# A later first conversion, closer conversions, three filling products and another order of banks in an attention and expert kernel

## The chip, the cores and the metric

The kernel runs on one core of one Trainium2 chip. The metric is the device time of one execution in microseconds (us). Five engines work side by side, each through its own queue in order: TensorE (PE, products), VectorE (DVE), ScalarE (ACT), GpSimd (POOL) and SyncE (SP, which here only issues DMAs). They meet by semaphores.

## What is computed

Three layers follow each other, all in float32, on 1152 tokens of 512 numbers. The reference, cut to what matters:

```python
# 1. attention, 2 batches x 8 heads, 1152 keys, 576 pooled queries
q_pool = q.reshape(B, H, S // 2, 2, D).mean(axis=3)
attn = softmax(q_pool @ k.T / sqrt(D));  x = attn @ v          # -> 1152 x 512
# 2. mixture of 8 experts, each token goes to its two best
noisy = x @ w_gate + log1p(exp(x @ w_noise)) * noise
top2 = np.argpartition(-noisy, 2, axis=1)[:, :2]               # softmax over the two
out[mask] += top2_w[mask, k, None] * (relu(x[mask] @ w1[e]) @ w2[e])
# 3. a dense layer pair, 512 -> 2048 -> 512, weights given in float64
h = x @ w_in;  g = np.where(h > 0, h, np.exp(np.minimum(h, 0)) - 1)
return (g @ w_out).astype(np.float32)
```

`w_in` and `w_out` come as float64. The chip has no float64, so the kernel turns them into float32 itself, bit by bit, in 32 pieces of 128x512 numbers.

## The kernel before

**Precision.** A product of two float32 matrices is made as three products of halves: each operand is split into a high part (rounded to the format that TensorE takes) and a low part (the rest). ACT makes the high part by a copy (`W.hi`, line 674; `xh`, line 727; `hh`, line 736), DVE or POOL the low part by a subtraction (`W.lo`, line 678; `xl`, line 728; `hl`, line 737).

**Attention (lines 171 to 386).** Eight units of two heads. The order of all steps is written out in a table of planned times, and steps that other parts of the kernel put in (`extra`, line 1034) are sorted among them. At its end stand, on PE, the transposition of the last query rows (`tl1`, line 363), which ACT copies (`tl1c`, line 367), a small product with the gate's weights (`tl2`, line 371), and on DVE the sum of its result into the gate's input (`tl2c`, line 375). PSUM has eight banks. The pool of attention has three under the tag `t` (the first that is asked for), four under `s` and one under `o`. The buffers of a tag are placed where the tag is first used, in that order, and a buffer in the next pool waits for the last reader of the bank that it takes over.

**The experts.** After attention a new PSUM pool is opened, with tags `a` (3 banks), `t` (2) and `o` (3). The first product of expert 0 for the first batch (`First.l1`, line 843, planned by `plan_first`, line 858) asks for an `a` bank first; so `a` lies on the three banks that attention had as `t`. Then each expert e has a first layer (`l1`, line 735, eight steps f of twelve products of 312 columns), a second layer (`l2t`, line 745, four steps of 24 products), and the transposition of the next expert's rows (`te`, line 726, in two pairs, `t` banks) between them. All steps are events of a `Line`: each has a planned time, the events are sorted by it, and every engine gets its instructions in that order. The planned times are no waits: an engine goes on as soon as its operands are there, but never past an instruction that waits. `V0` is the planned start of expert 0 and `D`=29.7 the planned length of one expert, so expert e starts at V0+29.7e. A step of the plan is called by its planned distance from V0 below ("at 16.5").

**A branch.** At 13.37 stands a conditional (line 559) for tokens that overflow an expert; every engine passes it, and the memory for the conversions is opened only behind it.

**Weights.** `plan_weight` (line 685) plans four loads of 512 KB on SP's queue (line 672, into six buffers), four high parts on ACT and four low parts on DVE or POOL for each half of an expert (its w1 or its w2).

**Conversions.** `plan_convert` (line 696) plans each of the 32 pieces, one every `CV[1]` from `CV[0]` on:

```python
    ln.at(t-3,load); ln.at(t,bits); ln.at(t+2,small); ln.at(t+8,store)
```

`load` (line 701) is a DMA of 512 KB on SP into one of two buffers; `bits` is four instructions on DVE (lines 705 to 708); `small` two on POOL (lines 711 and 712); `store` a DMA of 256 KB on SP (line 714) of the result to DRAM. Before, the first has bits at 16.5 and each next one 5.7 later, so the last has them at 193.2. On SP the store of conversion i stands just ahead of the load of conversion i+2, both in the same in-order queue as the loads of the experts' weights.

**The dense layers (lines 967 to 1009)** run when the experts are done, in three chunks of tokens; they read the converted weights from DRAM.

Of the kernel before, what the change touches and what calls it, by code (L numbers as in the profile page):

```python
# [4 lines left out]
FT=mybir.dt.float32; FR=mybir.dt.float32r; BF=mybir.dt.bfloat16; I32=mybir.dt.int32  # L5
# [143 lines left out]
def consts(tc, cp):  # L149
    nc=tc.nc  # L150
    c={}
    jp=cp.tile([128,128],I32,name="jp")
    nc.gpsimd.iota(jp,pattern=[[1,128]],base=0,channel_multiplier=-1)
    c['id']=cp.tile([128,128],FT,name="ident")
    nc.vector.tensor_scalar(c['id'],jp,0.0,None,op0=OP.is_equal)
    c['idr']=cp.tile([128,128],FR,name="identr")
    nc.vector.tensor_copy(c['idr'],c['id'])
    rw=c['rw']=cp.tile([128,8,80],FT,name="rw"); c['wd']=cp.tile([128,4,16],FT,name="wd")
    for r in range(2): nc.vector.tensor_copy(rw[64*r:64*r+64,:,0:64],c['id'][64*r:64*r+64,None,64*r:64*r+64].to_broadcast([64,8,64]))
    return c  # L160
# [520 lines left out]
def w2_src(w2, e, i): return ap(w2,e*512*1024+i*256*512,[[512,128],[128*512,2],[1,512]])  # L681
# [176 lines left out]
def plan_first(ln, F, pm, hp, ps, T):  # L858

    A={}  # L860
    def l1(f, b, c0=0, c1=4):
        F.l1(ps,f,b,c0,c1)
        A[b,f//3]=F.a
    for f in range(8): ln.at(T['l1']*f,l1,f,0)
    for i,n in enumerate((3,3,2)):
        ln.at(T['l1']*(3*i+n)+.02,lambda i=i,n=n: F.relu(hp,0,3*i,n,A[0,i])); ln.at(max(T['hl0']+.01*i,T['l1']*(3*i+n)+.03),lambda i=i,n=n: F.rest(0,3*i,n,A[0,i]))
    for j in range(5): ln.at(T['hot']+.001*j,F.ones,pm,j)
    for c in range(4): ln.at(T['mul']+.005*c,F.mul,ps,c); ln.at(T['mul']+.03+T['dm']*c,F.cut,hp,c)
    t=T['two']
    for f in range(3): ln.at(t+.001*f,l1,f,1,0,3)  # L870
    for f in range(3): ln.at(t+.01+.001*f,lambda f=f: (setattr(F,'a',A[1,0]),l1(f,1,3,4)))
    for f in range(3,8): ln.at(t+T['l1']*f,l1,f,1)
    for i,n in enumerate((3,3,2)):
        ln.at(t+T['l1']*(3*i+n)+.02,lambda i=i,n=n: F.relu(hp,1,3*i,n,A[1,i])); ln.at(t+T['l1']*(3*i+n)+.03,lambda i=i,n=n: F.rest(1,3*i,n,A[1,i]))
# [138 lines left out]
def build(tc, q, k, v, wg, wn, noise, w1, w2, win, wout, out):  # L1013
    nc=tc.nc
    with ExitStack() as es:
        def P1(n,b=1,st=es,**kw): return st.enter_context(tc.tile_pool(name=n,bufs=b,**kw))
        cp=P1("c"); dr=P1("dr",space=bass.MemoryType.DRAM)
        xs=dr.tile([OV0+OVN+NDUMP,512],FT,name="xs"); ys=dr.tile([NROW,512],FT,name="ys")
        ms=es.enter_context(ExitStack()); ms.enter_context(tc.manual_schedule())
        wf=[win,wout]  # L1020
        wide=win.dtype!=FT
        if wide: wf=[dr.tile([1<<20],FT,name=f"wf{i}") for i in range(2)]
        c=consts(tc,cp); g={}
        gk=P1("gk")
        scat=[]
        xe=ExitStack()
        X_=P1("X",st=xe,side="right")
        pm=P1("pm0",st=xe,side="right")
        g['ic']=pm.tile([128,HC],FT,name="icap")
        X=[X_.tile([128,5,512],FT,name=f"X{b}") for b in range(2)]  # L1030
        L=[cp.tile([128,5,16],FT,name=f"L{b}") for b in range(2)]
        F=First(tc,g,X,w1,xs,c['id'])
        gb=[]
        def extra(ps,ek,kk):
            psf=lambda: ps.tile([128,512],FT,tag="t",name="pg",bufs=TB)
            pss=lambda: ps.tile([128,1,512],FT,tag="s",name="pg",bufs=4)[:,0]
            def step():
                if not gb: gb.append(gating(tc,g,0,0,range(5),cp,gk,psf,X[0],L[0],xs,scat))
                next(gb[0],0)
            def late():  # L1040
                for b in range(2): nc.gpsimd.memset(L[b][64:128,4],0.0)
                ici=g['ic'].bitcast(I32)
                nc.gpsimd.iota(ici.rearrange("p (j n) -> p j n",j=2),pattern=[[1,2],[2,HC//2]],base=HC,channel_multiplier=0)
                nc.gpsimd.tensor_copy(g['ic'],ici)
                gate_consts(tc,cp,g)
            def swap():
                ek.close()
                F.open(P1("fw",st=xe,side="right"),kk)
            ld=lambda u: STEPS['load'][3 if u==7 else min(u,2)][0]+UU*u+.01
            ev=[(ld(2),lambda: consts2(tc,c,wg,wn)),(T0,late),(ld(3),late_loads(tc,g,cp,noise))]  # L1050
            ev+=[(ld(3+i//3),f) for i,f in enumerate(zero_fills(tc,g,cp,xs,ys))]
            ev+=[(t,step) for t in GATE]
            ev+=[(PRE['swap'],swap),(PRE['load'],F.load)]
            ev+=[((max(237.1,GATE[i+10]) if i<10 else PRE['split'])+.001*(i+1),lambda i=i: F.split(i)) for i in range(20)]
            for i in range(2): ev+=[(PRE['xt'][0]+.1*i,lambda i=i: F.xt(pss,i)),(PRE['xt'][1]+.1*i,lambda i=i: F.xh(i)),(PRE['xt'][2]+.1*i,lambda i=i: F.xl(i))]
            return ev
        attention(tc,c,X,L,q,k,v,extra,WARM)
        rp=P1("rp"); wp=P1("wp"); ps=P1("ps",space=PSUM); e2=es.enter_context(ExitStack())
        hp=P1("hp",st=e2)
        W=Weights(tc,wp,rp,1); ln=Line(); xp=Late(); cv=Late()  # L1060
        wt={}
        s1,s2=[128,4,1024],[128,8,512]
        psf=lambda: ps.tile([128,512],FT,tag="t",name="pg",bufs=2)
        gt=gating(tc,g,1,1,range(5),cp,gk,psf,X[1],L[1],xs,scat)
        for t in GT: ln.at(t,lambda: next(gt,0))
        ct=counts(tc,g,cp,psf)
        for t in CNT: ln.at(t,lambda: next(ct))
        plan_first(ln,F,pm,hp,ps,FIRST)
        V0=FIRST['two']+8*FIRST['l1']+.2-EX['l2']
        wt[0,1]=plan_weight(ln,W,s2,lambda i: w2_src(w2,0,i),2,*WP['a2'])  # L1070
        wt[1,0]=plan_weight(ln,W,s1,lambda i: w1_src(w1,1,i),1,V0+WP['b1'][0],V0+WP['b1'][1],WP['b1'][2],'vpvp')
        for i in range(4): ln.at(V0+TG+i,lambda: (next(gb[0],0),next(gt,0)))
        ln.at(V0+16,joint_tail,tc,g,cp)
        for e in range(1,9):
            t=V0+D*(e-1)
            if e>1:
                f=(lambda i,e=e: w1_src(w1,e,i)) if e<8 else (lambda i: win_src(wf[0],0,i))
                wt[e,0]=plan_weight(ln,W,s1,f,1,t+WP['1'][0],t+WP['1'][1],WP['1'][2],'vpvp',None,WP['1'][3])
            f=(lambda i,e=e: w2_src(w2,e,i)) if e<8 else (lambda i: wout_src(wf[1],0,i))
            wt[e,1]=plan_weight(ln,W,s2,f,2,t+WP['2'][0],t+WP['2'][1],WP['2'][2],'vpvv',None,WP['2'][3])  # L1080
        if wide:
            for i in range(32):
                plan_convert(ln,tc,(win,wout)[i//16],wf[i//16],i%16,cv,V0+CV[0]+CV[1]*i)
        box={}
        for e in range(8):
            plan_expert(ln,tc,e,V0+D*e,[wt.get((e,0)),wt[e,1]],c['id'],xs,ys,xp,hp,ps,None if e else Hs(F),box if e==7 else None)
        ln.run(V0+EX['l2']-.05)
        xe.close()
        if OVF: overflow(tc,g,w1,w2,xs,ys,c['id'],ps)
        W.p0.p=P1("wp0",side="right")  # L1090
        with e2:
            xp.p=P1("xp",st=e2); e3=e2.enter_context(ExitStack()); cv.p=P1("cv",st=e3,side="right")
            ln.run(V0+7*D+2)
            e3.close(); xr=P1("xr",side="right"); lp=P1("lp",st=e2)
            plan_last(ln,tc,g,V0+7*D,box,c['id'],ys,xp,hp,lp,ps)
            ln.run()
        xp=P1("xp2"); x2=P1("x2"); gp=P1("gp",2)
        ln=Line()
        wi=[wt[8,0],plan_weight(ln,W,s1,lambda i: win_src(wf[0],1,i),1,*MW[0],MW[2])]
        wo=[wt[8,1],plan_weight(ln,W,s2,lambda i: wout_src(wf[1],1,i),2,*MW[1],MW[3],last=x2)]  # L1100
        for ch in range(3):
            t=62*ch
            xt=plan_combine(ln,tc,g,ch,t-30 if ch else -2,(t-3.9,t-3.5) if ch else (-.2,-.2),c['id'],ys,xp,xr,ps,box['acc'])
            plan_moe2(ln,tc,ch,t,xt,wi,wo,out,gp,xp,ps)
        ln.run()
OVF=True; T0=20; TG=4.32; WARM=8; MW=((0,2,3),(12,14,3),'pppp','pppp'); CNT=(13.2,13.9); CV=(16.5,5.7)
PRE=dict(swap=237,load=446.2,split=446.3,xt=(581.65,582.,613.1))
GT=[0,.1,.2,.25,.26,.27,.3,.4,5.35,5.36]+[5.5+.01*i for i in range(11)]
FIRST=dict(l1=1.35,hl0=5.9,hot=5.4,mul=8.05,dm=.6,two=10.85)
WP={'a2':(-2.69,3,1.5,'vvvv',None,5.5),'b1':(5.23,9.87,3.81),'1':(-2.04,1.53,2.85,1.91),'2':(10.24,16.62,3.22,0.85)}  # L1110
# [31 lines left out]
```

## Time and profile before

| what | value |
|---|---|
| time, median of 3 runs | 814.61 us (811.88 to 817.9) |
| time of the profiled execution | 808.12 us |
| its span (first to last instruction) | 806.3 us, granted TensorE clock 0.994 |
| PE busy | 768.7 us (95%) |
| DVE busy | 560.9 us (70%) |
| ACT, POOL busy | 481.0 us (60%), 332.4 us (41%) |
| DMA moved | 119.41 MB, mean 148 GB/s |

All times in the rows are from the start of the span of that one execution. Attention ends near 304, the experts' second layers begin at 334 behind the branch, and the dense layers run from 601 to the end. Columns of a timeline: start in us, length in us, engine, line, operation, output <- inputs, shape, count; the brackets hold the idle time of the engine before the row and what ended it.

### The profile page before, as it was taken

The numbers are of one execution on the slowest core, as the hardware profiler recorded it, in microseconds if no ns is written. First come the engines' busy times: TensorE is split into PE (matmuls) and PEld (weight loads), VectorE is DVE, ScalarE is ACT, GpSimd is POOL, SyncE is SP. The second block draws the span as 40 slices with busy tenths as digits, with TensorE's granted clock in tenths as the row PEclk, the third lists the DMA queues.
The fourth block names the chain that finished last, engine by engine and source line by source line (L and its number), as shares of the span: only waits on it lengthen the run. The fifth ranks groups of instructions, "written<-read, shape, count | busy, mean of one in ns | idle before, by whom it ended". The sixth has DMA issues, their size and how long they took to land.

```text
span 806.3 us, 13467 instructions
## 1 busy us (share of the span) xinstructions
PE 768.7 (95%) x4891; PEld 706.1 (88%) x4891; DVE 560.9 (70%) x1134; ACT 481.0 (60%) x1109; POOL 332.4 (41%) x303
## 2 busy tenths in 40 slices
PE   6999999999999999978989999989999999999997
PEld 5898989998888888978989998889889999999996
DVE  6988898988999876595979879894555433243322
ACT  6988888989888874443545445444447334334432
POOL 4634051432520674365787777754519301000000
PEclk9999999999999999989999999999999999999999
DMA  8039466131102235568798797986634203001001
GB/s 255 2 109 268 133 235 213 45 108 37 50 30 106 91 88 219 149 236 265 272 305 284 284 321 263 317 257 220 228 90 164 78 1 105 1 14 39 1 1 40
DMA packets 51165, 119.41 MB, mean 148 GB/s; under 512 B 7725, under 2 KB 8749, under 8 KB 51097
## 3 DMA queue, kind: packets, MB, share of 16 engines
q1 hardware_dynamic: 48104, 108.96, 41.0%
q0 software_dynamic: 2912, 9.44, 3.6%
q8 instruction: 40, 0.66, 0.3%
q14 instruction: 29, 0.23, 0.1%
q10 hardware_dynamic: 80, 0.13, 0.0%
HBM read 82.55 MB, written 35.96 MB: 147 GB/s over the span
## 4 chain that ended last, share of the span: by engine, by line
PE 32%; DMA 11%; DVE 9%; issue 2%; POOL 2%; ACT 1%; SPq 1%; DVEq 0%; POOLq 0%; ACTq 0%
PE a L976 12%; PE o L994 12%; DMA raw<-in_moe_w_in_dram 4%; PE oe L745 4%; DMA raw<-in_moe_w_out_dram 3%; DVE wl L678 2%; DVE cvt L707 2%; PE ae L735 2%; DMA raw<-in_moe_w_dram 2%; DVE cvm L705 2%; DVE cvt L706 1%; POOL cvm L712 1%; DMA raw<-wf 1%; PE ac L926 1%; DVE cvt L708 1%
## 5 line engine op out<-in xcount | busy, mean ns | idle before, releaser
L297 ACT ACTIVATE p<-sp,m 128x384 f32<-128x384 f32 x216 | 124.9, 584 | 13.1 <-DVE m L289 12.9
L286 DVE TENSOR_REDUCE m<-sp 128x1 f32<-128x384 f32 x216 | 115.4, 551 | 19.0 <-PE sp L281 17.1
L674 ACT ACTIVATE wh<-raw 128x1024 fp32r<-128x1024 f32 x76 | 79.8, 1057 | 40.2 <-DMA raw<-in_moe_w_dram 34.0
L309 DVE TENSOR_TENSOR pl<-t_p,ph 128x512 fp32r<-128x512 f32 x144 | 96.8, 683 | 5.9 <-ACT ph L306 5.1
L678 POOL TENSOR_TENSOR wl<-raw,wh 128x1024 fp32r<-128x1024 f32 x32 | 84.2, 2640 | 30.8 <-ACT wh L674 29.5
L306 ACT ACTIVATE ph<-t_p 128x512 fp32r<-128x512 f32 x144 | 86.1, 603 | 16.8 <-PE t_p L303 11.4
L982 DVE SCALAR_TENSOR_TENSOR r<-m,a 128x384 f32<-128x384 f32 x48 | 26.6, 554 | 86.7 <-ACT m L981 86.6
L303 PE MATMUL t_p<-ident,p 128*128 128x128 f32 x576 | 83.2, 274 | 1.2 <-ACT xt L367 0.7
L281 PE MATMUL sp<-khl,qh 128*128 128x384 f32 x192 | 74.4, 388 | 4.9 <-ACT p L297 4.2
L303 PEld LDWEIGHTS t_p<-ident,p 128*128 128x128 f32 x576 | 67.9, 140 | 9.8 <-ACT xt L367 0.9
L711 POOL TENSOR_SCALAR cvm<-cvm 128x512 f32<-128x512 f32 x32 | 51.3, 1602 | 42.0 <-DVE cvm L705 42.0
L678 DVE TENSOR_TENSOR wl<-raw,wh 128x1024 fp32r<-128x1024 f32 x44 | 66.5, 1521 | 2.6 <-ACT wh L674 2.6
L281 PE MATMUL sp<-khl,ql 128*128 128x384 f32 x192 | 64.8, 338 | 0.0
L314 PE MATMUL o<-ph,vhl 128*128 128x512 f32 x144 | 63.8, 443 | 0.0
L980 ACT ACTIVATE m<-a 128x384 f32<-128x384 f32 x48 | 23.4, 488 | 64.3 <-PE a L976 64.3
L238 POOL TENSOR_SCALAR kr<-kraw 128x576 fp32r<-128x576 f32 x14 | 9.5, 676 | 125.0 <-PE t_k L245 125.0
L315 PE MATMUL o<-pl,vhl 128*128 128x512 f32 x144 | 57.4, 399 | 1.0 <-DVE pl L309 0.9
L712 POOL TENSOR_TENSOR cvm<-cvm,cvt 128x512 f32<-128x512 f32 x32 | 50.2, 1568 | 17.7 <-DVE cvt L708 17.1
L994 PE MATMUL o<-wh,g2h 128*128 128x512 f32 x144 | 56.7, 394 | 0.0
L994 PE MATMUL o<-wl,g2h 128*128 128x512 f32 x144 | 56.4, 391 | 0.0
L994 PE MATMUL o<-wh,g2l 128*128 128x512 f32 x144 | 56.3, 391 | 0.0
L985 DVE TENSOR_TENSOR g2l<-r,g2h 128x384 fp32r<-128x384 f32 x48 | 33.4, 696 | 28.4 <-ACT g2h L984 28.4
(268 smaller groups left out, 1932.2 us busy)
## 6 DMA issues: line engine op xcount, KB each, us to landing
raw<-in_moe_w_dram SPq DMA_DIRECT2D x60, 512.0 KB
raw<-in_moe_w_in_dram SPq DMA_DIRECT2D x16, 512.0 KB
wf<-cvm SPq DMA_DIRECT2D x32, 256.0 KB
raw<-in_moe_w_out_dram SPq DMA_DIRECT2D x16, 512.0 KB
raw<-wf SPq DMA_DIRECT2D x16, 512.0 KB
xs<-zrow SPq DMA_DIRECT2D x3, 1792.0 KB
xs<-zrow SPq DMA_DIRECT2D x2, 2560.0 KB
vraw<-in_v_dram SPq DMA_DIRECT2D x8, 576.0 KB
```

Source lines behind the costliest of these rows:

```text
L281: nc.tensor.matmul(sp[:,g,0:384],w,kh[:,h,384*(g0+g):384*(g0+g)+384],start=i==0,stop=i==len(ops)-1)
L286: nc.vector.tensor_reduce(m[:,x:x+1],s['s',j,x][:,:,0:384],axis=AX.XY,op=OP.max,negate=True)
L297: nc.scalar.activation(s['p',j][:,384*g0:384*(g0+nb)].rearrange("p (g n) -> p g n",g=nb),s.pop(('s',j,x))[:,:,0:384],AF.Exp,bias=m[:,3:4], ...
L303: nc.tensor.transpose(t[:,jj*128:jj*128+128],s['p',4*h+jj][:,kt*128:kt*128+128],ident)
L306: nc.scalar.activation(ph,s['tp',h,kt],AF.Copy)
L309: nc.vector.tensor_tensor(pl,s.pop(('tp',h,kt)),s['ph',h,kt].bitcast(FT),op=OP.subtract)
L314: nc.tensor.matmul(s['o',h],w,s.pop(('ph',h,kt)),start=kt==0,stop=False)
L674: s.tc.nc.scalar.activation(w[0][:,p['i']*p['n']:(p['i']+1)*p['n']],p['r'],AF.Copy)
L678: e.tensor_tensor(w[1][:,sl],p['r'],w[0][:,sl].bitcast(FT),op=OP.subtract)
L712: nc.gpsimd.tensor_tensor(m,m,s['f'].bitcast(FT),op=OP.mult)
L976: nc.tensor.matmul(a[:,0:384],wv[:,c,fs],xv[:,c],start=n==0,stop=n==11); n+=1
L994: nc.tensor.matmul(O[i],gv[:,ts],wv[:,f%8],start=f==0 and n==0,stop=f==15 and n==2)
```

## The change

The change has three parts. The first conversion's bits are planned at 22 and not at 16.5, and each next one 5.55 later and not 5.7; so the last has them at 194.05. Three products of the identity with itself are put on PE at the end of attention, into a bank of tag `s`, at 828.6 of attention's plan: `tl1` is planned before it, `tl1c` at 828.71 and `tl2` at 830.13 behind it. And ahead of the first product of expert 0 a tile of tag `o` and one of tag `t` are asked for and not used, so that in the new pool `o` takes the first three banks, `t` the next two, and `a` the last three.

```diff
     A={}
     def l1(f, b, c0=0, c1=4):
+        if b==0 and f==0: ps.tile([128,512],FT,tag="o",name="fo",bufs=3); ps.tile([128,512],FT,tag="t",name="ft",bufs=2)
         F.l1(ps,f,b,c0,c1)
         A[b,f//3]=F.a
...
             ev+=[(t,step) for t in GATE]
+            def fill():
+                w=pss()
+                for _ in range(3): nc.tensor.matmul(w[:,0:128],c['id'],c['id'],start=True,stop=True)
+            ev+=[(PRE['fill'],fill)]
             ev+=[(PRE['swap'],swap),(PRE['load'],F.load)]
...
-OVF=True; T0=20; TG=4.32; WARM=8; MW=((0,2,3),(12,14,3),'pppp','pppp'); CNT=(13.2,13.9); CV=(16.5,5.7)
-PRE=dict(swap=237,load=446.2,split=446.3,xt=(581.65,582.,613.1))
+OVF=True; T0=20; TG=4.32; WARM=8; MW=((0,2,3),(12,14,3),'pppp','pppp'); CNT=(13.2,13.9); CV=(22,5.55)
+PRE=dict(fill=828.6,swap=237,load=446.2,split=446.3,xt=(581.65,582.,613.1))
```

## Rows read from the trace of the kernel before

**Rows 1.** The page's chain that ended last, share of the span by engine.
```profile
PE 32%; DMA 11%; DVE 9%; issue 2%; POOL 2%; ACT 1%; SPq 1%; DVEq 0%; POOLq 0%; ACTq 0%
```

**Rows 2.** Busy time by stage: stretch, length, PE, PEld, DVE, ACT, POOL, clock, DMA.
```profile
346.00:356.00 10.00, 5.96 (x25) 5.73 (x24) 9.93 (x9) 3.23 (x6) 9.17 (x5) 0.66 0.60 216
...
350.30:355.90 5.60, 5.60 (x23) 5.60 (x24) 5.54 (x4) 2.15 (x4) 5.60 (x3) 0.51 0.56 191
...
366.00:546.00 180.00, 164.68 (x1147) 160.06 (x1147) 149.97 (x205) 84.72 (x146) 133.08 (x73) 0.99 0.87 290
```

**Rows 3.** PE's waits, 336 to 366 (first row) and 366 to 556: total, times, longest.
```profile
PE te L726 <- DVE xl L728: 4.0, 1, 4.0
...
PE ae L735 <- DVE hl L737: 5.4, 6, 1.4
PE oe L745 <- ACT hh L736: 4.8, 3, 2.8
PE oe L745 <- DVE hl L737: 3.2, 2, 1.9
PE te L726 <- DVE xl L728: 1.8, 2, 0.9
```

**Rows 4.** Timeline of DVE (four rows) and of POOL (last row), 343 to 355.
```profile
343.98 0.43 DVE L705 TENSOR_SCALAR cvm<-raw 128x512 int32<-128x512 int32 x1 [5.48 <-DMA raw<-in_moe_w_in_dram]
...
346.41 3.42 DVE L678 TENSOR_TENSOR wl<-raw,wh 128x1024 fp32r<-128x1024 f32 x2
...
349.75 0.86 DVE L728 TENSOR_TENSOR xl<-te,xh 128x312 fp32r<-128x312 f32 x2
...
352.26 2.60 DVE L706 TENSOR_SCALAR cvt<-raw 128x512 int32<-128x512 int32 x1
...
348.71 5.87 POOL L678 TENSOR_TENSOR wl<-raw,wh 128x1024 fp32r<-128x1024 f32 x2
```

**Rows 5.** Timeline of PE: second pair of transpositions, first layers of experts 1 and 7.
```profile
350.27 1.30 PE L726 MATMUL te<-ident,xe 104*128 104x104 f32 x6 [4.04 <-DVE xl L728]
...
357.11 0.73 PE L735 MATMUL ae<-xh,wh 128*128 128x312 f32 x4
...
559.12 0.73 PE L735 MATMUL ae<-xh,wh 128*128 128x312 f32 x4
```

**Rows 6.** Timeline of SP: first conversion's load and store.
```profile
337.44 0.45 SPq L701 DMA_DIRECT2D raw<-in_moe_w_in_dram  x1
...
348.77 0.33 SPq L714 DMA_DIRECT2D wf<-cvm  x1
```

**Rows 7.** Timeline of PE at the start of the span, and where attention ends.
```profile
2.88 3.78 PE L383 MATMUL t_w<-ident 128*128 128x128 f32 x16 [2.88 <-DVE ident L155]
...
300.46 1.50 PE L353 MATMUL t_v<-vraw,pt 128*128 128x128 f32 x12
...
302.74 0.27 PE L363 MATMUL t_l<-ident,X 64*128 64x64 f32 x1
303.33 0.29 PE L371 MATMUL t_l<-wd,xt 128*64 128x16 f32 x2 [0.31 <-ACT xt L367]
304.22 0.34 PE L848 MATMUL a<-x0h,w0h 128*128 128x168 f32 x1 [0.60 <-DVE L L375]
```

**Rows 8.** First instruction of the 32 conversions on DVE, and its waits for loads.
```profile
L705 DVE TENSOR_SCALAR cvm<-raw x32: 411/429/2425, 344.0 to 547.7; 128x512 int32<-128x512 int32 x32
...
DVE cvm L705 <- DMA raw<-in_moe_w_in_dram: 16.2, 8, 5.5
DVE cvm L705 <- DMA raw<-in_moe_w_out_dram: 13.0, 8, 3.5
```

**Rows 9.** SP's waits from 336 to 556, the longest in total.
```profile
SPq L714 <- POOL cvm L712: 109.4, 24, 8.1
```

**Rows 10.** The chain that ended last: two loads of conversions, one behind the other.
```profile
400.76 6.35 DMA raw<-in_moe_w_in_dram
...
412.82 7.51 DMA raw<-in_moe_w_in_dram
```

## The prediction

> **What bounds the kernel now.** I read the page's chain first. PE alone holds 32% of the span, DMA 11% and DVE 9% [rows 1]: so there is a stage in which PE doesn't set the pace. The table by stage finds it. Between 366 and 546, where the experts run, PE is busy 164.68 of 180 us, DVE 149.97, and the DMA engines 0.87 of the time at 290 GB/s [rows 2]. None of the three is free, none is always full. PE's waits say what ends its pauses: 15.2 us from 366 to 556 (5.4+4.8+3.2+1.8), always a low or high part that DVE or ACT made late, and ahead of that one pause of 4.0 us on xl [rows 3].
>
> That pause is the largest single one. DVE stood idle for 5.48 us, until 343.98, before the first conversion's first instruction, waiting for the load of its piece [rows 4]. That load was issued at 337.44, right behind the branch [rows 6], while DVE works in order: behind the conversion stand two low parts of weights (3.42 us, from 346.41) and only then the xl on which PE waits. So PE's second pair of transpositions came at 350.27 and not some 4 us before, and it paid twice: after the pause the granted clock is 0.51 from 350.30 to 355.90, that is 1.2 GHz and not 2.4 [rows 2, 5].
>
> From there on the conversions run in a loop of their own. A store waits for POOL, SP waits with it (24 times, 109.4 us in all [rows 9]), and behind the store stands the load of the conversion after next. Two such loads of the chain start at 400.76 and 412.82 [rows 10]: 12.06 us for a round of two, 6.03 us each, against 5.7 planned. DVE waits for 16 of the 32 loads, 29.2 us in all; 31 distances from 344.0 to 547.7 are 6.57 us each [rows 8]. PE gets through an expert in 33.7 us ((559.12-357.11)/6 [rows 5]) where the plan has 29.7: 33.7 times 5.7/29.7 is 6.46 us per conversion, so plan and loop go together.
>
> **The change part by part.**
>
> *First conversion later (16.5 to 22).* On DVE the order behind the branch was: bits 0, two low parts of weights, xl of the first pair, bits 1. It becomes: the two low parts, xl of the first pair, bits 0, xl of the second pair. So PE's second pair would start where the pause began, at 350.27-4.04 = 346.23. From it to expert 1's first layer PE took 6.84 us (350.27 to 357.11), 5.6 of them at half clock; at full clock that is 6.84-2.8 = 4.04, so the first layer would start at 350.3 and not at 357.11: 6.8 us [rows 2, 5].
>
> What is late next: on SP the load of conversion 0 moves behind two more weight loads of 512 KB (those planned at 16.66 and 16.68); these come earlier by that, the conversion's load some 1 us later. In flight 6.35 to 7.51 us [rows 10], it lands at 344.8 to 346, bits 0 start there, and the second pair's xl stands behind them. Bits take 2.43 us (343.98 to 346.41) alone and a pair of xl 0.86, but L706 took 2.60 us, some 2.2 more than its neighbour's 0.43, when POOL was at a low part of weights, until 354.58 [rows 4]. POOL's two low parts (5.87 us) then fall onto bits 0. So xl of the second pair ends between 348.1 (344.8+2.43+0.86) and 351.5 (346+2.43+2.2+0.86); PE needs it some 1.2 us into its first layer, at 351.5, in the third group of products. Cost 0 to 0.5 us for a semaphore's way; I take 0.2. The store of conversion 0 goes from 348.77 to some 351 to 353 and holds SP, but the load of conversion 1 and one weight load now stand ahead of it. Front gain: 6.6 us, bounds 4.0 (the clock falls anyhow, at another pause) and 6.8.
>
> The Trainium skill (GPSIMD Engine Reference, section 1) states that GpSimd shares its SBUF interfaces with VectorE, with contention when VectorE runs in a two-port mode or has two SBUF inputs. It speaks against this part, since bits 0 now meet POOL's weights; the 2.60 us agree. Were L705 held as well, by another 2.2 us, xl would end at 353.7 at the latest, 2.2 us late, and the sum below would be 3.0 and not 5.0.
>
> *Closer conversions (5.7 to 5.55).* New conversion i stands where old conversion i+1 stood, by 0.2+0.15i earlier: one conversion fewer lies ahead of PE at first, and the last one is planned 0.85 behind the old last. An expert of 29.7 thus holds 5.35 conversions and not 5.21. No instruction or byte is added; but both spacings lie under the loop's 6.03, so the loop is pressed harder. What 0.14 conversions more cost an expert: at least 0 if they fall into idle time; by DVE's own work 0.14 x 2.43 = 0.34 us; by the whole distance 0.14 x 6.57 = 0.92 us. Over the six experts from 1 to 7: 0, 2.0 or 5.5 us. I take 2.0: DVE, busy 83% of the stage, is the engine whose lateness ends most of PE's waits [rows 2, 3]. A gain is not excluded either: weights that leave one store earlier could end part of the 15.2 us of waits.
>
> *Filling products and banks.* The trace has tl1 at 302.74, tl2 at 303.33 after 0.31 us of idle, and expert 0's first product at 304.22 after 0.60 us, which DVE's read of tl2's bank ended [rows 7]. Six float32 products of 128 columns (twelve records) took 1.50 us: three take 0.67 to 0.75; the same instruction at the cold start took 3.78 us for eight, which bounds three at 1.42. They hide 0.31 us of idle and push tl2 on by 0.3 to 0.45 us (1.1 at most). In return the first product no longer waits: its bank was the `t` bank of tl2, and will be one of `s` or `o` whose readers are long done. It would start at 303.8: 0.4 us sooner, bounds -0.5 and 0.6. The gate's chain on DVE starts 0 to 0.1 us later, under products. PE has no pause from there to the branch, so the 0.4 us reach it.
>
> **Sum.** 6.6 - 2.0 + 0.4 = 5.0 us. Behind expert 7 PE has hardly a pause, so what is gained there arrives at the end. The profiled execution took 808.12 us with a span of 806.3; it would take 803.1 with 801.3. It lies 6.5 us under the median of the runs shown, 814.61; on the median 5.0 us less are 809.6.
>
> **The rivals.**
>
> *More than the front is kept (802.5).* Front and banks give 7.0, and with the conversion that is one further back the weights arrive earlier, so that a third of the 15.2 us of waits goes, 5.1: 12.1 us. For it: SP's queue is held by stores for 109.4 us. Against: the DMA engines are busy 0.87 of the stage as it is [rows 2, 9].
>
> *The loop sets the pace (815.3).* If a conversion takes its 6.57 us whatever stands around it, and bits 0 start at 346, the last starts at 346+203.7 = 549.7 and not 547.7, and PE is there 0.85 planned us (0.96 at its pace) further on, with 0.4 from the banks: 2.0-0.96-0.4 = 0.6 us slower, and the front's gain turns up as new waits. For it: 16 waits for loads. Against: the old mean contains the slow start itself.
>
> *PE pauses long enough for the clock to fall (826.4).* Place: bits that now stand ahead of the last hl of a first layer (conversion 3 at 38.6, ahead of hl 6 and 7 of expert 1). If their load is as late as DVE's longest waits (3.5 to 5.5 [rows 8]), PE stops for some 4 us before the second layer, and as after the 4.04 us pause loses 2.8 us more. [...] In all six experts: 16.8 us against the 5.0. Against it: of the pauses after 366 the longest is 2.8.
>
> *The banks don't do it (810.3).* If the first product still waits for tl2's reader, the filling only adds 0.3 and the 0.4 are missing.
>
> **How the numbers follow.** Chances: forecast 0.42, more kept 0.23, loop 0.19, clock 0.06, banks 0.10. 1% is 8.1 us, about what a measurement of this kernel can tell from no change. Faster by more (under 806.5): most of the second case and the forecast's edge, 0.26. Slower by more (over 822.8): the clock case and a little, 0.07. The rest, 0.67, is within 1%. The range from 802 to 816.5 holds the forecast, the loop and the banks with the run's spread, and nearly all of more kept; the likeliest case alone spans 807 to 812.
>
> **What would show it.** Right: no idle of DVE near 338 to 344 before L705; the second pair of transpositions straight behind the second layers, clock 1.00 from 346 to 356; expert 1's first layer near 350, expert 7's near 554; the first product of expert 0 straight behind tl2. The conversions' waits and PE's waits in the stage stay or grow by some 2 us. Wrong: a pause of 4 us at another place with a clock near 0.5 behind it; or expert 1 early but expert 7 at 559 again (the loop); or at 547 (more kept).

## The result, and the profile after

The changed kernel takes 806.09 us (median of five executions, 804.8 to 806.76) against 814.61 of the kernel before (five executions, 811.47 to 817.9). The ratio is 0.9897, 95% interval 0.9849 to 0.9944: 1% faster. 805 to 807 lies inside the range predicted and 3.5 us below the value. The profiled execution took 804.8 us with a span of 803.0, 3.3 us less than the one before (808.12). Throughout, a ratio and its interval leave out executions more than 1.5% above the fastest of their kernel, while a median holds all of them; that is why the two don't always move together.

First the changed kernel's busy time by stage; the columns are those of [rows 2].

```profile
346.00:356.00 10.00, 9.75 (x70) 9.26 (x69) 9.13 (x11) 6.14 (x11) 6.83 (x5) 1.00 0.62 218
350.30:355.90 5.60, 5.35 (x39) 4.91 (x38) 5.53 (x9) 3.23 (x6) 2.43 (x3) 1.00 0.39 116
366.00:376.00 10.00, 7.32 (x44) 7.07 (x43) 4.91 (x8) 3.70 (x6) 8.26 (x5) 0.87 1.03 323
366.00:546.00 180.00, 165.51 (x1140) 160.44 (x1139) 147.07 (x203) 83.69 (x142) 136.19 (x75) 0.99 0.88 293
```

From 346 to 356 PE is busy 9.75 us and not 5.96, at a granted clock of 1.00 and not 0.66: the pause and the half clock behind it are gone. From 366 to 546 little has changed in the sum, 165.51 us of PE against 164.68; but from 366 to 376 PE is busy 7.32 of 10 us at a clock of 0.87, which the section on the prediction comes back to. PE's timeline of the changed kernel says the same by its starts (compare [rows 5]):

```profile
346.44 0.70 PE L726 MATMUL te<-ident,xe 104*128 104x104 f32 x6
...
350.68 0.74 PE L735 MATMUL ae<-xh,wh 128*128 128x312 f32 x4
...
351.82 0.92 PE L735 MATMUL ae<-xl,wh 128*128 128x312 f32 x4
...
556.08 0.73 PE L735 MATMUL ae<-xh,wh 128*128 128x312 f32 x4
```

The second pair of transpositions stands straight behind the second layers, with no idle noted. Expert 1 starts 6.4 us earlier (350.68 for 357.11), expert 7 only 3.0 us (556.08 for 559.12). On DVE the order is the one that was worked out (timeline of DVE in the changed kernel, compare [rows 4]):

```profile
346.77 0.43 DVE L705 TENSOR_SCALAR cvm<-raw 128x512 int32<-128x512 int32 x1 [2.71 <-DMA raw<-in_moe_w_in_dram]
347.12 2.63 DVE L706 TENSOR_SCALAR cvt<-raw 128x512 int32<-128x512 int32 x1
349.78 0.98 DVE L707 SCALAR_TENSOR_TENSOR cvt<-raw,cvt 128x512 int32<-128x512 int32 x1
350.79 0.69 DVE L708 SCALAR_TENSOR_TENSOR cvt<-raw,cvt 128x512 int32<-128x512 int32 x1
351.40 0.87 DVE L728 TENSOR_TENSOR xl<-te,xh 128x312 fp32r<-128x312 f32 x2
```

DVE still waits for conversion 0's load, 2.71 us where it was 5.48, but now the first pair's xl is behind it. L706 is held to 2.63 us, from 347.12, while POOL is at its low parts (POOL's timeline, changed kernel), and the second pair's xl ends at 352.27.

```profile
344.50 4.96 POOL L678 TENSOR_TENSOR wl<-raw,wh 128x1024 fp32r<-128x1024 f32 x2 [5.90 <-ACT wh L674]
```

At attention's end the first product's wait did not go (timeline of PE in the changed kernel, compare [rows 7]):

```profile
302.97 0.27 PE L363 MATMUL t_l<-ident,X 64*128 64x64 f32 x1
303.17 0.94 PE L1056 MATMUL pg<-ident 128*128 128x128 f32 x6
304.04 0.29 PE L371 MATMUL t_l<-wd,xt 128*64 128x16 f32 x2
304.58 0.34 PE L848 MATMUL a<-x0h,w0h 128*128 128x168 f32 x1 [0.26 <-DVE L L375]
```

The first product of expert 0 still waits for L375 on DVE, and starts 1.61 us behind tl1 where it was 1.48. DVE's own timeline there shows what L375 stands behind, first in the changed kernel, then its last two rows in the kernel before:

```profile
303.51 0.42 DVE L331 TENSOR_TENSOR X<-t_c,r 128x256 f32<-128x256 f32 x1
303.85 0.22 DVE L336 TENSOR_TENSOR tm<-t_c,r 128x64 f32<-128x64 f32 x1
304.10 0.23 DVE L337 TENSOR_TENSOR L<-L,tm 128x64 f32<-128x64 f32 x1
304.36 0.16 DVE L375 TENSOR_TENSOR L<-L,t_l 64x16 f32<-64x16 f32 x1
```

```profile
303.87 0.22 DVE L337 TENSOR_TENSOR L<-L,tm 128x64 f32<-128x64 f32 x1
304.01 0.15 DVE L375 TENSOR_TENSOR L<-L,t_l 64x16 f32<-64x16 f32 x1
```

No row notes idle time: in the kernel before, L375 is the last of a queue that DVE works off behind the t_c products, 0.14 us behind the start of L337, while tl2 had ended at 303.62 (303.33+0.29). In the changed kernel the filling has pushed tl2 back, it ends at 304.33 (304.04+0.29), and L375 starts right behind it, 0.26 us behind L337: there tl2 itself ends last. That is where the 0.13 us come from.

The conversions run as before (L705 on DVE in the changed kernel, and below it SP's longest wait from 336 to 556, compare [rows 8, 9]): 31 distances from 346.8 to 545.4 are 6.41 us each, where they were 6.57.

```profile
L705 DVE TENSOR_SCALAR cvm<-raw x32: 414/428/2250, 346.8 to 545.4; 128x512 int32<-128x512 int32 x32
```

```profile
SPq L714 <- POOL cvm L712: 109.5, 26, 11.3
```

So the profiled pair explains 3.3 us by the front, less some of it given back. The medians differ by 8.5. The executions of the kernel before spread, those of the changed kernel don't; the experiments had to say why.

### The profile page after: what moved, and what is told of

Its sections match the earlier page's. It is cut to its first block, busy times and chain, and to the rows that moved or that the text cites. A ratio compares the mean times of both kernels' runs of the same rounds, so it can differ in the third digit from the quotient of the medians.

```text
span 803.0 us, 13488 instructions
## 1 busy us (share of the span) xinstructions
PE 769.2 (96%) x4897; PEld 706.0 (88%) x4897; DVE 557.9 (69%) x1134; ACT 480.7 (60%) x1109; POOL 334.0 (42%) x303
## 4 chain that ended last, share of the span: by engine, by line
PE 34%; DMA 10%; DVE 8%; POOL 2%; issue 2%; SPq 2%; ACT 1%; POOLq 0%; DVEq 0%; ACTq 0%
PE a L977 12%; PE o L995 12%; PE oe L745 5%; DMA raw<-in_moe_w_in_dram 4%; DMA raw<-in_moe_w_out_dram 3%; PE ae L735 2%; DVE cvt L707 2%; DVE cvm L705 1%; DVE wl L678 1%; POOL cvm L712 1%; DVE cvt L706 1%; DMA raw<-wf 1%; DVE cvt L708 1%; PE ac L927 1%; DMA raw<-in_moe_w_dram 1%
## 5 line engine op out<-in xcount | busy, mean ns | idle before, releaser
L678 DVE TENSOR_TENSOR wl<-raw,wh 128x1024 fp32r<-128x1024 f32 x44 | 63.0, 1441 | 2.6 <-ACT wh L674 2.6
```

Source lines behind the costliest of these rows:

```text
L678: e.tensor_tensor(w[1][:,sl],p['r'],w[0][:,sl].bitcast(FT),op=OP.subtract)
```

## The experiments

The kernel before ran beside them each time; it appears in the table by its median on the same chip. "Low clock" counts executions whose mean granted clock over the span is below 0.986 (a bound chosen from what was seen: the five executions of the result lie at 0.987 to 0.996). e7 has no result; e9 makes the same change. One of e3's twelve executions took 1511.61 us at a clock of 1.00, and one of the 35 of the kernel before beside e9 to e12 took 1511.85; nothing here explains these two.

```
kernel                                      median  before  ratio [95%]              low clock
e1  kernel before again                     816.05  818.30  1.0023 [0.9975, 1.0070]   7 of 12
e2  conversions (22, 5.55) alone            810.79  818.30  0.9940 [0.9889, 0.9991]   7 of 13
e3  first conversion later, alone           813.51  818.30  1.0008 [0.9959, 1.0057]   5 of 12
e4  closer conversions (16.5, 5.55) alone   819.19  818.30  1.0044 [0.9987, 1.0101]   7 of 12
e5  whole change again                      806.02  815.23  0.9911 [0.9875, 0.9948]   0 of 12
e6  filling alone                           810.66  815.23  0.9986 [0.9944, 1.0028]   2 of 12
e8  whole, spacing 5.7                      806.06  815.23  0.9905 [0.9868, 0.9942]   1 of 12
e9  whole without filling                   810.50  816.78  0.9964 [0.9917, 1.0011]   7 of 12
e10 banks alone                             813.18  816.78  1.0000 [0.9959, 1.0042]   5 of 12
e11 whole without banks                     804.97  816.78  0.9914 [0.9877, 0.9951]   1 of 12
e12 whole, filling one step earlier         806.14  816.78  0.9934 [0.9905, 0.9963]   0 of 12
e13 whole, filling in mid-attention         807.55  817.98  0.9939 [0.9905, 0.9973]   1 of 12
```

**The kernel before again, and the conversions alone.** e1 is the kernel before with an unused constant. e2, e3 and e4 change the planning of the conversions and nothing else.

In e2:

```diff
-CV=(16.5,5.7)
+CV=(22,5.55)
```

In e3, with CV as before:

```diff
-                plan_convert(ln,tc,(win,wout)[i//16],wf[i//16],i%16,cv,V0+CV[0]+CV[1]*i)
+                plan_convert(ln,tc,(win,wout)[i//16],wf[i//16],i%16,cv,V0+CV[0]+CV[1]*i+(5.5 if i==0 else 0))
```

In e4:

```diff
-CV=(16.5,5.7)
+CV=(16.5,5.55)
```

> The kernel before once more, nothing changed in what it does. Its one profile showed 808.12 us, its timed runs 811 to 818, while the changed kernel's runs lie within 2 us. Theory A: the profile was a lucky execution; in others further pauses of PE of some 3 us behind late conversion loads let the granted clock fall, so the mean clock is below 0.994 (each 0.01 of it is 16 us at half clock, 8 us lost) and the span 810 to 816. Theory B: the extra time lies outside the span or is spread over all stages with the same clock. Expect 811 to 818, a profile that differs from the first one in the stage from 336 to 556 alone if A holds.

> Both numbers of the conversions changed, no filling products, no other banks. My theory: all of the gain is here, so the time is that of the changed kernel, 805 to 807 (ratio 0.988 to 0.992), expert 1's first layer at 350.3 to 350.7, and expert 0's first product 1.48 us behind the start of the last transposition, not 1.61. Rival, the filling and banks matter through the clock or through the order of banks later on: 808 or more.

> Only conversion 0 is planned 5.5 later (bits at 22.0, just ahead of conversion 1 at 22.2); the other 31 keep their times. My theory: the pause ahead of the second pair of transpositions and the half clock behind it go (6.6 us at expert 1), and nothing is pressed closer, except that two conversions now stand side by side: 807 to 810. Rival, the loop of conversions sets the pace: the whole is given back by expert 7, 813 to 816.

> Spacing 5.55 from the old start 16.5, so the last conversion is planned at 188.55. My theory: the first pause stays (4.0 us, half clock behind it) and 0 to 5.5 us are added by more conversions per expert, 2.0 taken: 814.6 to 820, 816.6. Rival, the loop sets the pace: the last bits come when they came, with PE 4.65 planned us (5.3) further back: 820. Rival, closer conversions help by themselves: under 812.

e1 says how well the kernel before agrees with itself: within half a per cent by the interval, with single executions from 807 to 832 us. e2 is faster by 0.6%, but spreads like the kernel before. Its profiled execution was the longest of its thirteen, 833.04 us: PE was never idle long where the old pause had been, but expert 1's first layer came only at 377.25, because the granted clock was 0.50 from 306 until past 356 (PE by stretch, e2: length, PE, clock, DMA):

```profile
306.00:336.00 30.00, 30.00 (x127) 0.50 0.37 133
336.00:346.00 10.00, 10.00 (x62) 0.50 0.09 37
346.00:356.00 10.00, 10.00 (x48) 0.50 0.01 2
```

e3 gains nothing that can be measured: with only conversion 0 moved it meets conversion 1, and PE gets its pause one step later. Its timeline on PE:

```profile
345.56 0.70 PE L726 MATMUL te<-ident,xe 104*128 104x104 f32 x6
...
350.98 0.45 PE L735 MATMUL ae<-xl,wh 128*128 128x312 f32 x2
354.67 1.02 PE L735 MATMUL ae<-xl,wh 128*128 128x312 f32 x2 [3.24 <-DVE xl L728]
```

So moving the head alone only moves the pause. e4 keeps the old pause (4.0 us on xl) and shows neither gain nor loss outside its interval. Its trace has the fall of e2, which none of my cases held: the granted clock fell already at the end of attention. The same is seen in e9 below.

**The filling.** e5 repeats the whole change; e6 adds the filling alone to the kernel before; e9 takes it out of the changed kernel:

```diff
-            def fill():
-                w=pss()
-                for _ in range(3): nc.tensor.matmul(w[:,0:128],c['id'],c['id'],start=True,stop=True)
-            ev+=[(PRE['fill'],fill)]
```

> The whole change once more, on one chip with the next three. Theory (the filling products keep the granted clock up behind the end of attention): every execution within 4 us, 804 to 808 us, mean clock 0.987 to 0.997; the kernel before spreads again from 807 to over 830 on the same chip. Rival (the narrow spread of the first five executions was luck): some executions at 815 us or more, with a mean clock below 0.985.

> The three filling products alone; conversions and banks as before. Theory: the fastest execution is like that of the kernel before (806 to 808 us, since the products themselves cost under 0.2 us), and the slow ones of 815 us and more are gone: median 807 to 810, granted clock 1.00 in 304 to 336 us. Rival (the conversions or the banks make the spread narrow): spread and median as the kernel before on the same chip, 813 to 819.

> The change without the filling products: later and closer conversions, and the other order of banks. Theory: executions spread from 804 to over 820 us, some with a mean clock below 0.98, median 808 to 814, as with the conversions alone; the first product of the expert stage starts 1.4 to 1.7 us behind the product ahead of tl2, behind VectorE's copy at L375. Rival (the banks keep the clock up, or spare the wait): all within 4 us of 805, or the first product straight behind tl2.

e5 came out nearly as the theory had it, from 801.79 to 808.42 us and with no low clock. e6 came close: low-clock executions are rare, the median is 4.6 us under that of the kernel before, the highest is 817.2; but the ratio, which leaves the slowest out, shows no gain on its own. e9 has the spread again, 803.2 to 816.6, and seven of its twelve executions stand above the highest of e5; its ratio is 0.9964, where e5 has 0.9911; the intervals of the two overlap, so that it is the count of low clocks, 7 of 12 against 0 of 12, that tells them apart. What they lose is seen in its trace: PE's busy time by stretch around the end of attention (length, PE, clock, DMA), without filling (e9):

```profile
304.00:306.00 2.00, 1.40 (x12) 0.94 1.03 381
306.00:320.00 14.00, 14.00 (x75) 0.50 0.27 106
320.00:324.00 4.00, 4.00 (x17) 0.64 0.59 223
324.00:336.00 12.00, 12.00 (x104) 1.00 0.52 179
```

Ahead of it PE had the two pauses of [rows 7]; here is e9's timeline of PE from them to the fall:

```profile
303.86 0.29 PE L371 MATMUL t_l<-wd,xt 128*64 128x16 f32 x2 [0.31 <-ACT xt L367]
304.75 0.34 PE L848 MATMUL a<-x0h,w0h 128*128 128x168 f32 x1 [0.60 <-DVE L L375]
...
305.60 0.27 PE L848 MATMUL a<-x0h,w0l 128*128 128x168 f32 x1
305.71 0.34 PE L848 MATMUL a<-x0l,w0h 128*128 128x168 f32 x1
305.85 0.42 PE L848 MATMUL a<-x0h,w0h 128*128 128x168 f32 x1
```

A product of 168 columns takes 0.27 us up to 305.6 and 0.42 from 305.85 on; from 306 to 320 PE is busy all the time at 0.50, that is 1.2 GHz. The second layers' first pair of transpositions starts at 350.33 and not at 342.19 as in the changed kernel (PE's timeline, first e9, then the changed kernel): 8.1 us, on an execution of 812.58 us.

```profile
350.33 0.70 PE L726 MATMUL te<-ident,xe 104*128 104x104 f32 x6
```

```profile
342.19 0.70 PE L726 MATMUL te<-ident,xe 104*128 104x104 f32 x6
```

The traces of e2, e4 and e10 show the same fall at the same place; those of the kernel before, e1 and e3, with the same pauses, don't. So it happens in some executions and not in others. None of the seven traces with the filling has it.

**The banks.** e10 is the kernel before with the line that asks for two unused tiles, e11 the changed kernel without it:

```diff
+        if b==0 and f==0: ps.tile([128,512],FT,tag="o",name="fo",bufs=3); ps.tile([128,512],FT,tag="t",name="ft",bufs=2)
```

> The other order of banks alone. Theory: nothing; spread (807 to over 825 us) and median (813 to 819) as the kernel before on the same chip, and the first product waits for L375 as before, for 0.5 to 0.7 us. Rival (the prediction's step): it starts straight behind tl2, 0.5 us sooner, and executions below a mean clock of 0.98 are gone.

> The change without the other order of banks. Theory: as the changed kernel, median 805 to 807, all executions between 801 and 809 us. Rival (banks and filling are needed together): spread to over 815 us.

Both as the theory had it. In e10 the first product still waits 0.61 us for L375; its timeline row:

```profile
304.57 0.34 PE L848 MATMUL a<-x0h,w0h 128*128 128x168 f32 x1 [0.61 <-DVE L L375]
```

By the order in which the tags are first asked for, the bank of that product moved; no view of the profile names banks. The product waits for the same instruction of DVE with both orders, so asking for the tiles in another order does not end the wait; why it is there stays open. e11 is as fast as the whole.

**The spacing.** e8 is the changed kernel with the old spacing:

```diff
-CV=(22,5.55)
+CV=(22,5.7)
```

> The change with the old spacing of 5.7 instead of 5.55: later conversions, filling and banks. Theory as in the prediction, that the closer spacing costs: expert 1's first layer within 0.6 us of the changed kernel's 350.7, expert 7's 1 to 3 us earlier than its 556.1, time 1 to 3 us below the changed kernel's. Rival (the spacing costs nothing, or gains): the time within 0.7 us of it, or 1 us and more above it.

The median is that of e5 (806.06 and 806.02), the ratios differ by 0.0006: no price of the closer spacing is seen in the time, but each interval is some 3 us wide to either side, so that a price of 2 us could not be seen there. In the traces expert 1 to expert 7 takes 201.4 us in e8 and 202.3 in e5 (first layers at 351.35 and 552.72, 350.75 and 553.08), but 205.4 in the first profiled execution of the change. Over all traces but e3's it is 201.0 to 204.0 us in the five with a spacing of 5.7 (the kernel before, e1, e6, e8, e10; mean 202.0) and 202.3 to 208.0 in the eight with 5.55 (the changed kernel, e2, e4, e5, e9, e11 to e13; mean 205.3). With one execution of each that speaks for a price, and doesn't prove it.

**Where the filling stands.** e12 and e13 are the changed kernel with another due time of the filling, 700.6 and 200.6. In e12:

```diff
-PRE=dict(fill=828.6,swap=237,load=446.2,split=446.3,xt=(581.65,582.,613.1))
+PRE=dict(fill=700.6,swap=237,load=446.2,split=446.3,xt=(581.65,582.,613.1))
```

In e13:

```diff
-PRE=dict(fill=828.6,swap=237,load=446.2,split=446.3,xt=(581.65,582.,613.1))
+PRE=dict(fill=200.6,swap=237,load=446.2,split=446.3,xt=(581.65,582.,613.1))
```

> The whole change, but the three filling products issued in the middle of attention, where TensorE has no pause, and none between the last products of attention. Theory (they work by where they stand): as the change without them: spread from 804 to over 820 us, some with a mean clock below 0.98, median 808 to 814. Rival (their place does not matter): all within 4 us of 805.

> The whole change, with the filling products issued early in attention, among the score products (due time 200 instead of 828.6). Due time 700 had moved them by only one step, from behind the product ahead of tl2 to in front of the t_c products, and left the pauses at 0.31 and 0.25 us. Here the pauses should be 0.31 and 0.60 us again. Theory (it is the work next to these pauses, and shorter pauses, that keep the clock up): spread from 804 to over 815 us, some executions with a mean clock below 0.985, median 808 to 813, as without filling. Rival (the place of the products does not matter, only that they, or their buffer, are there): all within 5 us of 806.

e12 went against the theory, though less than its expectation says: the products had moved only from behind tl1 to ahead of t_c. e13 is the fairer test. There the pauses are back (PE's timeline of e13), and so is the clock of 1.00 behind them (PE by stretch, e13, same columns as for e9):

```profile
304.54 0.29 PE L371 MATMUL t_l<-wd,xt 128*64 128x16 f32 x2 [0.31 <-ACT xt L367]
305.44 0.34 PE L848 MATMUL a<-x0h,w0h 128*128 128x168 f32 x1 [0.61 <-DVE L L375]
```

```profile
306.00:320.00 14.00, 14.00 (x115) 1.00 0.41 150
320.00:324.00 4.00, 4.00 (x33) 1.00 0.87 314
```

Eleven of its twelve executions lie between 804.9 and 808.7 us, one fell to a clock of 0.957. So my theory, that the filling works by shortening these pauses, fell, though e13's one trace by itself would not show it, since e1's is clean too: the same products 75 us earlier (at 228.2 to 228.9) do nearly all of it. With the filling, wherever it stands, 5 of 77 executions had a low clock (e5, e6, e8, e11 to e13 and the five of the result); without it 38 of 73 (e1 to e4, e9, e10), and 70 of the 117 executions of the kernel before that ran beside all twelve. With like conversions it is 3 of 65 against 14 of 25 where they are later and closer (e2 and e9 without), and 2 of 12 (e6) against 12 of 24 in e1 and e10. That the filling does it is shown; how, is open. Where it stands ahead of t_c it delays what follows by some 0.7 us (in e12 the t_c products start 0.67 us behind the filling's first), in the changed kernel by no more than the 0.13 us seen above; and it takes one more buffer of tag `s`, so that the tiles behind it turn to other banks. A kernel with the buffer and no products, or with the delay and no buffer, would have told these apart; neither was tried.

## Why the prediction was right, and where it was not

The value, 809.6, was 3.5 us too high and the range held the time. That was luck in part: 806.09 lies outside the 807 to 812 of the likeliest case, and just below 806.5, where the chance was put at 0.26. The profiled pair gained 3.3 us and not 5.0, and the median got the rest from a term that the sum held at nothing, the filling's effect on the clock. The terms one by one:

*The front, 6.6 us: right.* The second pair of transpositions came at 346.44 (346.23 worked out), expert 1's first layer at 350.68 (350.3), 6.4 us earlier than before. Conversion 0's bits began at 346.77, 0.8 us behind the late end of what was worked out. The 2.2 us that POOL's low parts were to add fell on L706 as said, 2.63 us in all, and the second pair's xl ended at 352.27, 0.8 us behind the late end as well. It cost PE next to nothing: the group of products that needs it, at 351.82, took 0.92 us where its neighbours take 0.74. The sentence on VectorE and GpSimd in the Trainium skill (GPSIMD Engine Reference, section 1) would have made the sum 3.0 if L705 were held too; L705 took its 0.43 us, so that case did not come. (In e3, where bits 0 started at 346.08, it was L705 that took 2.58 us and L706 its 0.42.)

*Closer conversions, -2.0 us: open in size, and not by the mechanism it gave.* The profiled execution gave back 3.4 us between expert 1 and expert 7 (6.4 to 3.0). The step had spread the loss over six experts; 2.9 us of it go in expert 1 alone. Expert 2's first layer comes at 388.20 where it came at 391.71, and experts 2 to 7 then take 167.9 us (167.4 before). In expert 1 PE stops for 2.68 us ahead of the second layer, and behind it the granted clock is 0.50 from 374 to 376; the kernel before has 1.00 there. PE waits for hh, and ACT had stood ahead of that hh at a high part of weights whose load came late (rows of PE and of ACT, changed kernel; last row, PE in the kernel before):

```profile
372.70 0.41 PE L745 MATMUL oe<-hh,wh 128*128 128x312 f32 x1 [2.68 <-ACT hh L736]
388.20 0.73 PE L735 MATMUL ae<-xh,wh 128*128 128x312 f32 x4
```

```profile
371.27 1.06 ACT L674 ACTIVATE wh<-raw 128x1024 fp32r<-128x1024 f32 x1 [2.82 <-DMA raw<-in_moe_w_dram]
372.24 0.41 ACT L736 ACTIVATE hh<-ae 128x312 fp32r<-128x312 f32 x1
```

```profile
391.71 0.73 PE L735 MATMUL ae<-xh,wh 128*128 128x312 f32 x4
```

A low clock within expert 1, somewhere between 366 and 391, stands in the traces of e4, e5, e8, e9 and e11 to e13 as well, behind pauses of PE, and in none of the kernel before, e1, e6 and e10, whose conversions have the old start and the old spacing. So it comes with the later row (e8, old spacing) and with the closer one (e4, old start), and takes back a part of what the front gains. What the spacing adds to it is not shown: by the times of e8 and e5 nothing, by the traces some 3 us. The conversions' own distance went to 6.41 us, so the rival by which the loop sets the pace is out. "More kept" is out by its mechanism: PE's waits from 366 to 556 are 14.4 us where they were 15.2, not a third less. These are the waits of the changed kernel in that stretch:

```profile
PE oe L745 <- ACT hh L736: 5.1, 3, 2.7
PE oe L745 <- DVE hl L737: 3.9, 2, 2.0
PE ae L735 <- DVE hl L737: 3.2, 5, 1.5
PE te L726 <- DVE xl L728: 1.4, 2, 0.9
PE ae L735 <- DVE xl L728: 0.8, 2, 0.4
```

*Filling and banks, +0.4 us: the step that failed, twice.* The step said that with the banks moved "the first product no longer waits". It does, for the same L375, and starts 0.13 us later behind tl1 than before: by the path alone the term is -0.13, as the rival "the banks don't do it" had it in sign. The three products took 0.94 us, more than the 0.67 to 0.75 worked out and less than the bound of 1.42, and tl2 was pushed on by 0.48 us. And the step priced the filling as work only. What it is worth is the clock: about half of the executions without it have a low mean clock, few with it do. In four of the seven traces without it the clock falls from 306 on, which costs 8.1 us in e9 and some 27 in e2 (expert 1 at 377.25 for 350.68). Median against median it is worth 4.5 us (810.50 of e9 to 806.02 of e5, while the kernel before beside them had 816.78 and 815.23; e11 and e12, beside e9 on the same chip, have 804.97 and 806.14), and 4.6 us where it is put alone into the kernel before (e6).

*The fall of the clock* stood among the rivals, behind a pause of some 4 us ahead of expert 1's second layer. A fall came at that place, behind 2.68 us, from a late load of weights and not from bits ahead of hl, and not in all six experts. The rival took a longest pause of 2.8 us as speaking against it; yet the kernel before itself has a clock of 0.50 from 544 to 546 behind just that pause:

```profile
543.72 0.63 PE L745 MATMUL oe<-hh,wh 128*128 128x312 f32 x1 [2.78 <-ACT hh L736]
```

The other place, the end of attention, no case named: in the traces of e2, e4, e9 and e10 the clock falls there behind some 0.3 and 0.6 us.

*From the profiled execution to the median.* The sum of 5.0 us was moved onto a median that holds executions with a low clock. Without the filling that nearly holds: e2 and e9 have medians of 810.8 and 810.5 for 809.6 predicted, 7.5 and 6.3 us under the kernel before on their chips. The further 4 us or so are the filling's. Why the profile of before could not show it: its profiled execution was one with a clean clock, 6.5 us under its own median; that distance was in the text, and no step asked where it came from.

## What to carry to other kernels

When the profiled execution lies well under the median, ask first what the other executions lose: compare the mean clock of each with its time, and find the place where the clock falls. Here it lay behind short pauses ahead of a dense stage, though it is not shown that these pauses make it fall. Products that cost 0.1 us on the path were worth about as much in the median as a scheduling fix of 6 us, of which the next stage gave part back by a pause of its own. A first conversion that waits for its load belongs behind the work that PE waits for, and in e3 it did not help to move it without the rest of its row.

## What was not expected of the hardware

TensorE's granted clock fell to 0.50 within 1.1 us of the restart behind two pauses of 0.31 and 0.60 us (e9: restart at 304.75, first long product at 305.85), and stayed there from 306 to 320, in which PE was busy 14.00 of 14 us; in e2 it stayed from 306 to 356, in which PE was never idle; behind the 4.04 us pause of [rows 5] it was low for 5.6 us only. The Trainium skill ("TensorE: Matmul & The Clock Gate", Part 1) says that the monitor behind the clock runs on without regard to the kernel, so that the same kernel differs from execution to execution. No run here shows the monitor; e9 and e1, two kernels with the same pauses, differ in that way, 0.50 and 1.00 behind them. No run here shows why three products 75 us earlier change how often it happens.
